# 32 columns of numerators: interleaved with the denominator sums, or in a round of their own

## The chip, the core and the metric

The kernel runs on one core of one Trainium2 chip. The core has a matrix engine (TensorE, PE in the profile, with its weight loads as PEld), a vector engine (VectorE, DVE), an activation engine (ScalarE, ACT), GpSimd (POOL) and SyncE (SP), each with an instruction queue of its own; they meet through semaphores. The metric is the device time of one execution in microseconds (us); lower is better. Times with two decimals in this document are starts within the span of the profiled execution.

## The reference

```python
def phi(x):                                     # per head, 8 x 8 products
    a = einsum('rd,bhsd->bhsr', S1, x)
    b = einsum('rd,bhsd->bhsr', S2, x)
    return einsum('bhsi,bhsj->bhsij', a, b).reshape(..., 64)
q_p, k_p = phi(q), phi(k)                       # q, k, v: 4 batches, 4 heads, 1088 tokens, 32 wide
kv  = einsum('bhsf,bhsd->bhfd', k_p, v)
z   = sum(k_p, axis=2)
num = einsum('bhsf,bhfd->bhsd', q_p, kv)
den = einsum('bhsf,bhf->bhs', q_p, z)[..., None] + 1e-06
x   = (num / den) as (4352 tokens, 128)
out = (sigmoid(x @ w_gate) * (x @ w_val)) @ w_out    # 1536 wide in between
```

All is float32. The attention part is linear in the tokens: each head needs one 64 x 32 matrix `kv` and one vector `z` of 64; then a numerator (32 values) and a denominator (one value) for each token.

## The kernel before, in words

**The feed-forward part is the long one.** The result of the attention lies in `xT`, 128 partitions (4 heads x 32) by 4352 tokens. The tokens are cut into eight chunks of 512 and a last one of 256. For each chunk `w1` makes twelve waves (`wave`, L544), each of 128 of the 1536 columns for gate and value; ScalarE takes the sigmoid (L552), VectorE multiplies (`glu`, L587), and the product with `w_out` follows some waves later as `prod` (L381), for which GpSimd makes sums of tokens (`tsum`, L371). For the chunks in the middle the weights are split in 64-column halves, so the profile shows those matmuls as 128*64.

**The attention of the batches 1 to 3 is slipped in between the waves.** The order on every engine is written out by hand. The function `slot` issues one wave and what has become due behind it; the list `plan` says at which wave each step of a batch stands. The steps of one batch are: transposes of k and q, features (`kps`, `qcomp`, `spread`, `outer`, `qmult`), `kv_all`, `ndt` (weights of the numerators, `ND`), `weights_z` (weights of the denominators, `ZW`), and last `parts(b)`, the step that this case is about. It stands in one slot for each of the three batches.

**The step `parts(b)`** does this:

1. `den_j` (L1026): eight matmuls `sum_j` (L1032), 64 rows by 32 columns of weights, 160 columns of data, into the PSUM tile `denj`. `pi` is the half of the rows (0 to 63, 64 to 127) and also the half of `denj`, which has two banks; `x` picks one of four groups of 32 output partitions. Between them stand eight numerator matmuls (L1268) of 32 columns, also into `denj`, columns 160 to 191. While `sum_j` uses the one half of the rows, the numerator beside it uses the other. Then VectorE multiplies `denj` by `A8` into `PD` (`pd`, L1047).
2. `glu()` for the wave before, on VectorE, behind `pd`.
3. The other 512 columns of numerators: eight matmuls (L1268) into the PSUM tile `nps`, copied to SBUF by ScalarE (`num`, L1285).
4. `den_i` (L1053): two matmuls of 128 rows by 64 columns on `PD`, back into columns 0 to 159 of the first bank of `denj`. They wait for `pd`.
5. `turn_den` and the rest on VectorE: transpose (`dTi`, L1065), reciprocal, transposes, and three multiplications into `xT` (L1302), the last of them of the 32 columns.

Each float32 matmul is two passes in the trace, each with its own weight load, so the eight 512-column matmuls are "x16". Tiles of 64 rows by 32 columns are eight separate parts of the array here, two halves of rows by four groups of columns.

The PSUM pool `ps2` has one buffer (tag "two"), two banks. `denj` lives in it, and so do `kps`, `kvz` and `ndps` of other steps: a new tile of that tag has to wait for all readers of the tile before it.

## Time and profile before

| | |
|---|---|
| median of 3 runs | 290.91 us (290.83 to 291.48) |
| profiled execution | 291.36 us, of which 289.3 us are the span of the instructions |
| granted TensorE clock | 1.0, all slices |
| TensorE busy | 283.5 us, 98% of the span |
| VectorE, GpSimd, ScalarE busy | 170.8, 159.6, 106.6 us |
| share of the chain that ended last on TensorE | 97% |
| first weight load of `parts(1)`, `parts(2)`, `parts(3)` | 72.44, 129.35, 193.57 us |

The 2.06 us between the span and the time of the execution lie around the instructions. The three steps `parts` look alike to 0.02 us in the trace, so the first stands for all. Ends of matmuls are modelled by the profiler: a matmul's duration contains the time in which its columns run in and the time in which the array empties, and the next one on the same part of the array starts before that end.

### The profile page before, as it was taken

Reading aid. Unit: us, or ns where it says so; the run is one execution under the profiler, and the core shown is the slowest. Engines: PE = TensorE matmul, PEld = TensorE weight load, DVE = VectorE, ACT = ScalarE, POOL = GpSimd, SP = SyncE. Lnnn points to the kernel's source line nnn. Section 1 sums busy time; section 2 is a strip of 40 time slices with the busy share of each in tenths; the row PEclk is TensorE's granted clock in tenths of the full one; section 3 lists DMA queues with packets and bytes.
Section 4 is the critical chain, followed back from the end, with each engine's and each line's share of the span. In section 5 each row is a group of like instructions: output and inputs, shape, how many; then the busy total and the mean of one; then the engine's idle time right before and its main releaser. Section 6 shows DMA issues by size and latency. Waiting matters only on the chain.

```text
span 289.3 us, 5786 instructions
## 1 busy us (share of the span) xinstructions
PE 283.5 (98%) x2260; PEld 134.9 (47%) x2260; DVE 170.8 (59%) x294; ACT 106.6 (37%) x215; POOL 159.6 (55%) x222
## 2 busy tenths in 40 slices
PE   8799999999999999999999999999999999999995
PEld 4454433354444444544444444444444444444685
DVE  6987788946738547668346385767245223522571
ACT  3688833222334322533234222522243223421341
POOL 2566673667466377372665396483564646555200
PEclk9999999999999999999999999999999999999999
DMA  7995541665600386442000683010001100020012
GB/s 216 343 361 120 111 155 42 164 147 135 186 11 2 77 187 162 105 156 37 0 1 6 157 162 128 2 28 10 0 3 18 18 2 0 3 35 1 0 17 40
DMA packets 28890, 24.22 MB, mean 84 GB/s; under 512 B 18560, under 2 KB 24064, under 8 KB 28864
## 3 DMA queue, kind: packets, MB, share of 16 engines
q1 hardware_dynamic: 25888, 22.10, 30.1%
q10 hardware_dynamic: 2976, 1.77, 2.1%
q8 instruction: 17, 0.28, 0.4%
q14 instruction: 9, 0.07, 0.1%
HBM read 20.60 MB, written 3.26 MB: 82 GB/s over the span
## 4 chain that ended last, share of the span: by engine, by line
PE 97%; ACT 1%; DVE 1%; issue 0%; POOL 0%
PE wave L544 61%; PE prod L381 22%; PE moeout L425 4%; PE moeout L451 2%; PE warm L301 2%; PE kvz L900 1%; PE nps L1268 1%; PE kps L681 1%; PE cqps L827 1%; PE nps L1101 0%; PE dps L1082 0%; PE denj L1053 0%; PE denj L1032 0%; ACT asb L798 0%; DVE qp L807 0%; PE ndps L965 0%
## 5 line engine op out<-in xcount | busy, mean ns | idle before, releaser
L544 PE MATMUL wave<-xT,w_sb 128*64 128x512 f32 (+3 forms) x820 | 201.9, 566 | 0.0
L552 ACT ACTIVATE sg<-wave 128x512 f32<-128x512 f32 x102 | 60.9, 597 | 158.6 <-PE wave L544 152.6
L587 DVE TENSOR_TENSOR g<-wave,sg 128x512 f32<-128x512 f32 x96 | 66.1, 688 | 88.2 <-ACT sg L552 87.6
L371 POOL TENSOR_TENSOR tsum<-g,tsum 128x256 f32<-128x256 f32 x84 | 68.4, 815 | 71.6 <-DVE g L587 71.5
L544 PEld LDWEIGHTS wave<-xT,w_sb 128*64 128x64 f32 (+1 forms) x820 | 71.3, 140 | 72.8 <-issue 53.0
L371 POOL TENSOR_TENSOR tsum<-g 128x256 f32<-128x256 f32 x84 | 66.4, 791 | 22.6 <-DVE g L587 22.0
L381 PE MATMUL prod<-tsum,ws 128*64 128x256 f32 x252 | 68.3, 380 | 0.0
L381 PE MATMUL prod<-g,w_sb 128*64 128x256 f32 x168 | 50.2, 380 | 0.0
L381 PEld LDWEIGHTS prod<-tsum,ws 128*64 128x64 f32 x252 | 34.0, 137 | 13.1 <-issue 9.7
L381 PEld LDWEIGHTS prod<-g,w_sb 128*64 128x64 f32 x168 | 22.7, 137 | 30.0 <-issue 25.8
L381 PE MATMUL prod<-tsum,w_sb 128*64 128x256 f32 x84 | 25.1, 380 | 0.0
L381 PE MATMUL prod<-g,ws 128*64 128x256 f32 x84 | 25.0, 379 | 0.0
L162 POOL TENSOR_TENSOR head<-head,tail 128x384 int32<-128x384 int32 (+1 forms) x13 | 13.2, 1021 | 4.4 <-DVE head L157 4.4
L381 PEld LDWEIGHTS prod<-g,ws 128*64 128x64 f32 x84 | 11.5, 137 | 5.7
L425 PE MATMUL moeout<-g,w_sb 128*128 128x512 f32 (+1 forms) x28 | 12.4, 600 | 0.0
L381 PEld LDWEIGHTS prod<-tsum,w_sb 128*64 128x64 f32 x84 | 11.3, 137 | 1.3 <-issue 1.0
L760 DVE TENSOR_TENSOR kp<-kab 128x1152 f32<-128x1152 f32 (+2 forms) x10 | 10.7, 1082 | 0.0
L580 DVE TENSOR_TENSOR g<-wave,sg 128x512 f32<-128x512 f32 x6 | 7.0, 1172 | 6.1 <-ACT sg L552 4.6
L880 DVE TENSOR_TENSOR qp<-qp,bq 128x1152 f32<-128x1152 f32 (+1 forms) x7 | 10.1, 1444 | 0.0
L493 DVE TENSOR_TENSOR res<-prod,other 128x256 f32<-128x256 f32 x14 | 6.0, 425 | 6.3 <-ACT other L484 4.8
L141 POOL TENSOR_SCALAR head<-cap 128x384 f32<-128x384 f32 (+1 forms) x13 | 6.3, 487 | 5.0 <-ACT cap L140 5.0
L152 ACT ACTIVATE tail<-w_in,two__157 128x384 f32<-128x384 uint32 (+1 forms) x12 | 7.3, 614 | 0.0
(132 smaller groups left out, 200.2 us busy)
## 6 DMA issues: line engine op xcount, KB each, us to landing
qp<-dq SPq DMA_DIRECT2D x7, 576.0 KB
bq<-dq SPq DMA_DIRECT2D x14, 288.0 KB
kq<-in_k_dram SPq DMA_DIRECT2D x3, 544.0 KB
kq<-in_q_dram SPq DMA_DIRECT2D x3, 544.0 KB
w_in<-in_moe_w_out_dram SPq DMA_DIRECT2D x6, 256.0 KB
w_in<-in_moe_w_gate_dram SPq DMA_DIRECT2D x5, 256.0 KB
w_in<-in_moe_w_val_dram SPq DMA_DIRECT2D x5, 256.0 KB
v<-in_v_dram SPq DMA_DIRECT2D x8, 144.0 KB
```

Source lines behind the costliest of these rows:

```text
L141: nc.gpsimd.tensor_scalar(out=self.head.bitcast(F32), in0=self.cap, scalar1=122880.0, scalar2=2.0**-15, op0=ALU.min, op1=ALU.max,)
L152: nc.scalar.activation(out=self.tail, in_=self.lo, func=ACTF.Identity, bias=two, scale=2.0**-51)
L162: nc.gpsimd.tensor_tensor(out=self.head, in0=self.head, in1=self.tail.bitcast(I32), op=ALU.add)
L371: nc.gpsimd.tensor_tensor(out=t[:, u], in0=in0, in1=in1, op=ALU.subtract)
L381: nc.tensor.matmul(out=out, lhsT=lhsT, rhs=rhs, start=start, stop=stop, skip_group_check=True)
L425: nc.tensor.matmul(out=moe["acc"][d], lhsT=w_sb[:, 2, j, d], rhs=g[:, jj], start=(j == 0), stop=(j == NJ - 1),)
L544: nc.tensor.matmul(out=wv[d, which, jj * tw + o : jj * tw + o + tp], lhsT=w_sb[:, which, j0 + jj, d], rhs=xT[:, t0 + o : t0 + o + tp], sta ...
L552: nc.scalar.activation(out=sg, in_=wv[:, 0], func=ACTF.Sigmoid)
L580: nc.vector.tensor_tensor(out=g.rearrange("p (j u s y) -> p j y u s", j=2, u=2, y=4), in0=wv[:, 1].rearrange("p (j y u s) -> p j y u s", j ...
L587: nc.vector.tensor_tensor(out=g, in0=wv[:, 1], in1=sg, op=MUL)
L760: eng.tensor_tensor(out=KP[b][:, pi, j0:j1].rearrange("p j m (i l) -> p (j m) i l", i=R), in0=bass.AP(tensor=a0.tensor, offset=a0.offset, ...
L880: nc.vector.tensor_tensor(out=q0, in0=q0, in1=half(BQ[b], n), op=MUL)
```

## The change

The 32-column numerators leave `den_j` and become a round of their own behind the 512-column ones. `den_j` is left with its eight `sum_j`. The function `numerators` issues all eight matmuls of one kind, in the order head, then half of the rows. In `parts` a new tile `nps2` of the tag "two" is taken after `den_j`; the 32-column numerators go to its columns 160 to 191, `den_i` to its columns 0 to 159, and `turn_den` and the last multiplication into `xT` read it in place of `denj`.

```diff
     def den_j(b):
         t = ps2.tile([P, 2, 512], F32, tag="two", name="denj")
-        rest = t[:, :, WD : WD + 32]
-        def sum_j(pi, x):
+        for pi in range(2):
             rows = slice(64 * pi, 64 * pi + 64)
-            nc.tensor.matmul(
-                out=t[32 * x : 32 * x + 32, pi, :WD],
...
-        for x in range(4):
-            sum_j(0, x)
-            numerator(b, rest, x, 1, True)
-        for x in range(4):
-            sum_j(1, x)
-            numerator(b, rest, x, 0, True)
+            for x in range(4):
+                nc.tensor.matmul(
+                    out=t[32 * x : 32 * x + 32, pi, :WD],
...
         nc.vector.tensor_tensor(out=PD[b], in0=t[:, :, :WD], in1=A8[b], op=MUL)
-        return t
...
+    def numerators(b, t, rest):
+        for h in range(H):
+            for c in range(2):
+                rows = slice(64 * c, 64 * c + 64)
+                q1 = QP[b].rearrange("p (n h w) -> p n h w", n=2, h=H)[rows, :, 2 * (h % 2) + h // 2]
+                nc.tensor.matmul(
+                    out=t[32 * h : 32 * h + 32, c],
+                    lhsT=ND[b][rows, 32 * h : 32 * h + 32],
+                    rhs=q1[:, 1, W1 - 32 :] if rest else q1[:, :, : W1 - 32],
...
     def parts(b):
-        t2 = den_j(b)
+        den_j(b)
         glu()
         t = psm.tile([P, 2, 512], F32, tag="wave", name="nps")
-        for h in range(H):
-            for c in range(2):
-                numerator(b, t, h, c, False)
+        numerators(b, t, False)
...
         nc.scalar.copy(out=num, in_=t)
-        turn_den(b, den_i(b, t2[:, 0, :WD]))
+        t = ps2.tile([P, 2, 512], F32, tag="two", name="nps2")
+        numerators(b, t[:, :, WD : WD + 32], True)
+        turn_den(b, den_i(b, t[:, 0, :WD]))
...
-            for u0, u1, x in ((0, 8, num[:, :, 256 * n : 256 * n + 256]), (8, tn, t2[:, :, WD : WD + 32])):
+            for u0, u1, x in ((0, 8, num[:, :, 256 * n : 256 * n + 256]), (8, tn, t[:, :, WD : WD + 32])):
```

In the program as built, TensorE has, per batch, 8 `sum_j`, 8 matmuls of 512 columns, 8 of 32 columns and the 2 of `den_i`, in this order; it had 8 `sum_j` and 8 of 32 columns alternating, 8 of 512 columns and the 2 of `den_i`. The wait for `pd` (VectorE) stands at the first 32-column matmul of `nps2`, where it stood at the first of `den_i`. No engine has an instruction more or less; the other engines' orders and every DMA are as they were.

More of the change, by code (lines that the diff above doesn't have):

```diff
@@ L1027, in den_j @@
         t = ps2.tile([P, 2, 512], F32, tag="two", name="denj")
-        rest = t[:, :, WD : WD + 32]
-        def sum_j(pi, x):
+        for pi in range(2):
             rows = slice(64 * pi, 64 * pi + 64)
-            nc.tensor.matmul(
-                out=t[32 * x : 32 * x + 32, pi, :WD],
-                lhsT=ZW[b][rows, 4 * (x % 2) : 4 * (x % 2) + 4].rearrange("p x i -> p (x i)"),
-                rhs=B8[b][rows, (W1 - WD) * (x // 2) : (W1 - WD) * (x // 2) + WD],
-                start=True,
-                stop=True,
-            )
-        for x in range(4):
-            sum_j(0, x)
-            numerator(b, rest, x, 1, True)
-        for x in range(4):
-            sum_j(1, x)
-            numerator(b, rest, x, 0, True)
+            for x in range(4):
+                nc.tensor.matmul(
+                    out=t[32 * x : 32 * x + 32, pi, :WD],
+                    lhsT=ZW[b][rows, 4 * (x % 2) : 4 * (x % 2) + 4].rearrange("p x i -> p (x i)"),
+                    rhs=B8[b][rows, (W1 - WD) * (x // 2) : (W1 - WD) * (x // 2) + WD],
+                    start=True,
+                    stop=True,
+                )
         PD[b] = sbA.tile([P, 2, WD], F32, tag="pd", name="pd", bufs=1)
         nc.vector.tensor_tensor(out=PD[b], in0=t[:, :, :WD], in1=A8[b], op=MUL)
-        return t
     def den_i(b, dps):
@@ L1263, in part01 @@
         late.append(dn(0, 1)(later=True))
-    def numerator(b, t, h, c, rest):
-        rows = slice(64 * c, 64 * c + 64)
-        q1 = QP[b].rearrange("p (n h w) -> p n h w", n=2, h=H)[rows, :, 2 * (h % 2) + h // 2]
-        nc.tensor.matmul(
-            out=t[32 * h : 32 * h + 32, c],
-            lhsT=ND[b][rows, 32 * h : 32 * h + 32],
-            rhs=q1[:, 1, W1 - 32 :] if rest else q1[:, :, : W1 - 32],
-            start=True,
-            stop=True,
-        )
+    def numerators(b, t, rest):
[7 more added lines that the diff above has]
+                    rhs=q1[:, 1, W1 - 32 :] if rest else q1[:, :, : W1 - 32],
+                    start=True,
+                    stop=True,
+                )
     def parts(b):
-        t2 = den_j(b)
+        den_j(b)
         glu()
         t = psm.tile([P, 2, 512], F32, tag="wave", name="nps")
-        for h in range(H):
-            for c in range(2):
-                numerator(b, t, h, c, False)
+        numerators(b, t, False)
         num = sbA.tile([P, 2, NJK, 2, F], F32, tag="kp", name="num", bufs=1)
```

## The prediction, made before the result was known

> **What bounds the kernel now.** I read first the page: busy times, the granted clock, and the chain of work that ended last.

> ```profile
> span 289.3 us, 5786 instructions
> ...
> PE 283.5 (98%) x2260; PEld 134.9 (47%) x2260; DVE 170.8 (59%) x294; ACT 106.6 (37%) x215; POOL 159.6 (55%) x222
> ...
> PEclk9999999999999999999999999999999999999999
> ...
> PE 97%; ACT 1%; DVE 1%; issue 0%; POOL 0%
> ```

> TensorE is busy in 98% of the span, the chain is TensorE for 97%, and its clock is granted in full. So a change of the end is, to first order, the change in the time that TensorE's own stream needs. Second, the chain between 70 and 80 us, in order of time (start, length, what).

> ```profile
> 70.79 1.72 PE wave L544 x8
> 72.51 0.18 PE denj L1032 x4
> ...
> 72.98 1.09 PE nps L1268 x16
> 74.07 0.42 PE denj L1053 x4
> 74.50 0.86 PE prod L381 x8
> 75.36 1.72 PE wave L544 x8
> ```

> From wave to prod nothing but TensorE: the step `parts` costs 1.99 us (72.51 to 74.50), three times 0.7% of the execution. Only what changes between the first `denj` pass and `prod` can count. Third, therefore, the timeline of that stretch (start, length, engine), asked for in narrow windows.

> ```profile
> 72.44 0.10 PEld L1032 LDWEIGHTS denj<-b,zw 64*32 64x32 f32 x1 [0.81 <-DMA v<-in_v_dram]
> 72.44 0.32 PE L1032 MATMUL denj<-b,zw 64*32 64x160 f32 x1
> ...
> 72.45 0.21 PE L1268 MATMUL denj<-qp,nd 64*32 64x32 f32 x1
> ...
> 72.80 0.59 PE L1268 MATMUL nps<-qp,nd 64*32 64x512 f32 x1
> ...
> 72.93 1.14 PE L1268 MATMUL nps<-qp,nd 64*32 64x512 f32 x15
> 73.21 0.49 DVE L1047 TENSOR_TENSOR pd<-denj,a 128x320 f32<-128x320 f32 x1 [1.83 <-PE denj L1032]
> ...
> 74.00 0.20 PEld L1053 LDWEIGHTS denj<-pd,head 128*64 128x64 f32 x4 [0.84 <-DVE pd L1047]
> ```

> The last line names `pd` as what `den_i` waited for. But `pd` ended at 73.21 + 0.49 = 73.70, and a TensorE load starts about 0.05 behind the VectorE instruction it waits for (`qT` ends at 14.18, the load of `cqps` starts at 14.23). From 73.75 on `pd` held nothing up. What did is the array: the last pass of `nps` has its modelled end at 74.07, and `den_i`, whose tile has another shape (128*64 after 64*32), loads 0.07 before it, just as the first `denj` load at 72.44 stands 0.07 before the modelled end of the wave (72.51). So `pd` has 0.25 us to spare now. The next answer, the second passes of `nps`, and one on all passes of `denj` give the durations:

> ```profile
> 73.23 0.84 PE L1268 MATMUL nps<-qp,nd 64*32 64x512 f32 x8
> ```

> ```profile
> L1032 PE MATMUL denj<-b,zw x48: 292/296/322, 72.4 to 193.9; 64*32 64x160 f32 x48
> ...
> L1268 PE MATMUL denj<-qp,nd x48: 188/193/214, 72.4 to 193.9; 64*32 64x32 f32 x48
> ```

> A pass of 512 columns lasts 0.59, one of 32 columns 0.19: 0.40 for 480 columns, 0.83 ns a column. So columns run for 0.43 (512), 0.13 (160) and 0.03 (32), and 0.16 of each duration is the array emptying. The last columns of `nps` are in at 74.07 - 0.16 = 73.91, and `den_i` follows 0.09 later. I follow the time of the last column before `den_i`, T = 73.91; the change in T, times three, is the change of the kernel.

> **The change, part by part.**

> *Front: 16 short passes leave `denj`.* Each of the eight parts of the array now takes two `sum_j` passes and two short ones. The first `nps` pass starts at 72.80 on the upper half of the rows; the other fifteen wait for the lower half until 72.93, and that sets T. On the lower half two short passes come first (72.45 and, 0.05 later, 72.50), then `sum_j` at 72.60 and 72.74 (0.13 of columns each), then `nps`. Without the short passes `sum_j` of the lower half can start at the earliest behind the four loads of the upper half, which come about 7 ns apart, two passes each: 72.47 to 72.50. Then `nps` gains 0.10 to 0.13. At the latest it starts at 72.60 as now, because its own wait (for the second half of `B8`, one of the two waits is a semaphore instruction of 0.05) or the second passes of the upper half (from 72.57) hold it: gain 0. A loss is possible as well: without the alternation the halves could run one after the other, and the lower half would start when the upper one's columns are in, 72.57 + 0.13 = 72.70: 0.10 later. The short passes did run beside `sum_j` of the other half in the trace, so parts of the array do start independently; I take a gain of 0.07, and keep -0.13 and +0.10 as ends.

> *Back: the 16 short passes stand behind `nps`.* They use the same eight parts and the same tile shape as `nps`, so there is no second emptying of the array between them. On the part that ends last, two more passes follow: 2 x 0.03 of columns, and the start of the first and of the second, 0.01 to 0.02 each (two short passes on one part stand 0.03 to 0.05 apart in `denj`). This is 0.06 at least and 0.10 at most, if the passes of the other parts run beside them, as the short passes of `denj` do at some 10 ns apart. A gain is excluded, since these columns can only come after `nps`. The far end: the round one pass after the other. The nearest row for that is `kvz`, 72 passes of 64 columns in 1.14 (the chain at 58.42): 0.016 each, 16 of them 0.25, and the first load, 0.10, not covered because it stands behind the wait for `pd`: 0.35. I take 0.09, near the `denj` row because that is the same tile shape with the same data, and keep 0.06 and 0.35.

> *The wait for `pd` moves ahead of the round.* Behind it on TensorE's queue stand the round, `den_i`, `prod` and the next wave. `pd` would be done at 73.70 as now, or up to 0.13 earlier with the front; the loads could start at 73.75. The part of the array that ends last is busy with `nps` until 73.91 - 0.07 = 73.84. So the wait is covered, by 0.09; the loads of the eight matmuls at 7 ns each use 0.05 of it. If `pd` came later than that, every 0.01 would cost 0.01 per batch. Cost taken: nothing, covered by the second passes of `nps`.

> *The tile `nps2`* waits for `pd` as the only reader of `denj`, the same wait. The next tile of the tag is needed only by the next batch's `kps`; after the last batch by the last chunk.

> *Other engines.* `num` (ScalarE) starts behind `nps`, so up to 0.07 earlier. `dTi` and the chain into `xT` move with `den_i`, by some 0.02. The last write to `xT` ends at 78.79; the first wave that reads these tokens starts at 79.92, its load at 79.71. That leaves 0.9 us. In batches 2 and 3 four waves lie between. POOL, SP and all DMAs keep their orders: nothing.

> *The sum.* Per batch -0.07 + 0.09 + 0 = +0.02, for three +0.06. The profiled execution, 289.3 + 2.06 around it = 291.36, becomes 291.42; it stands 0.45 above the median of the runs shown, so on the median: 290.97, rounded 291.0.

> [...]

> **The rivals.**

> *Slower: the round runs in series behind the wait.* If the first load of the round isn't covered (0.10) and its passes come at the pace of `kvz` (0.25), T is 0.35 - 0.07 = 0.28 later per batch, 0.84 in all: 291.75, or +0.29%. It decides from 0.19 per batch on. For it: nothing can be loaded ahead across the wait for `pd`, and the profile has no short round that stands alone. Against it: 32 short and long passes in 0.49.

> *Faster: the front is bound by the number of passes.* If `denj` is bound by passes and not by columns, half of the 32 passes is half of 0.49, so 0.25 per batch gained and 0.06 paid behind: -0.57 in all, 290.3. For it: the long and the short passes stand mixed at one pace. Against it: on the lower half the chain of starts accounts for no more than 0.13.

> *`pd` ends last.* It starts 0.14 behind the modelled end of the last `sum_j`, where `dTi` starts 0.05 behind `den_i`; so 0.09 are unexplained, perhaps its DMA waits. If that slack grew by 0.1 the cover would be gone: +0.1 per batch, 291.3; no change that can be told.

> That the round isn't placed where the change says can be left out: TensorE's order as built shows it.

> **How the numbers follow.** A measurement of this kernel can tell about 0.2% from no change, 0.58 us (its own runs spread from 290.83 to 291.48). The sum of my terms with nearer ends lies between -0.07 and +0.10 per batch, -0.2 and +0.3 in all, inside that bound. Chances: forecast 0.60 and `pd` last 0.08, both within 0.2%; in series 0.22, slower; bound by passes 0.10, faster. The far corner, halves in series in front and passes in series behind (+0.45 per batch, 292.3), is left out of the range, which reaches from the faster rival to the slower one, with 0.1 of each inside: 290.4 to 291.8. The forecast's own range is 290.6 to 291.4.

> **What would show it.** Right, if in the profile after: the first `den_i` load stands 1.50 to 1.65 us behind the first `denj` load (now 1.56); `nps`'s fifteen passes start 0.39 to 0.49 behind it; the short passes start within 0.15 and the first of them no later than 1.40 behind it; `pd` ends before the last `nps` columns are in. Wrong, if the first short load stands more than 0.1 behind both `pd` and the last columns of `nps`, if the short passes spread over 0.25, or if a wave waits for `xT`.

## The result, and the profile after

The changed kernel is a little faster, in the first comparison by 0.2 to 0.5%: 290.21 us (median of 14 runs, 290.00 to 290.75) beside 291.10 for the kernel before (14 runs on the same chip, 290.80 to 296.05). The ratio is 0.9965, with a 95% interval of 0.995 to 0.998; it is taken over fast executions alone, without the slow one of 296.05 us. A second comparison gave medians of 290.43 and 291.12 us and a ratio of 0.9987 (0.9973 to 1.000); the kernel before, run once more unchanged, gave 0.9994 (0.9984 to 1.0005). The forecast was a loss of 0.06 us.

First the page of the kernel after: span, busy times, shares of the chain that ended last.

```profile
span 288.4 us, 5785 instructions
...
PE 282.6 (98%) x2260; PEld 134.5 (47%) x2260; DVE 170.8 (59%) x294; ACT 106.6 (37%) x215; POOL 159.6 (55%) x222
...
PE 97%; DVE 1%; issue 0%; ACT 0%
```

TensorE is the bound as before, with 0.9 us less of busy time and a span 0.9 us shorter. The one instruction fewer (5786 before) is a wait for a semaphore in TensorE's stream. Then the chain of waits of the kernel after between 70 and 80 us (start, length, what).

```profile
70.43 1.72 PE wave L544 x8
72.14 0.43 PE denj L1029 x16
72.58 0.95 PE nps L1259 x27
73.53 0.42 PE nps L1042 x4
73.95 0.86 PE prod L381 x8
74.81 1.72 PE wave L544 x8
```

From the first `denj` to `prod` it is 73.95 - 72.14 = 1.81 us, where it was 1.99: 0.18 less. The wave, `prod` and the wave after it last what they lasted. The timeline of that stretch, in narrow windows (start, length, engine; buffer numbers are left out of names, so `nps` is also `nps2`; L1259 are the numerators, L1042 is `den_i`):

```profile
72.07 0.18 PEld L1029 LDWEIGHTS denj<-b,zw 64*32 64x32 f32 x16 [0.81 <-issue]
72.24 0.29 PEld L1259 LDWEIGHTS nps<-qp,nd 64*32 64x32 f32 x16
...
72.37 0.64 PE L1259 MATMUL nps<-qp,nd 64*32 64x512 f32 x8
...
72.69 0.49 DVE L1037 TENSOR_TENSOR pd<-denj,a 128x320 f32<-128x320 f32 x1 [1.67 <-PE denj L1029]
...
73.23 0.19 PEld L1259 LDWEIGHTS nps<-qp,nd 64*32 64x32 f32 x16 [0.70 <-DVE pd L1037]
73.46 0.20 PEld L1042 LDWEIGHTS nps<-pd,head 128*64 128x64 f32 x4
```

The eight first passes of the long numerators start together at 72.37, 0.30 behind the first load, within 0.05. Before, one started 0.36 behind the first load and the others from 0.49 on. The short round's loads stand at 73.23, and `den_i` follows at 73.46.

The step's length, from its first load to the first load of `den_i`, is the measure in all that follows, since it is alike to 0.002 us in all three batches: **1.562 us before, 1.382 after**. Three times 0.180 is 0.54 us, 0.19% of the execution. The spans differ by 0.9. The other 0.36 were there before the first wave: it starts at 14.53, and before at 14.90. In the kernel before, TensorE was slower at the start: the trace's record of the full clock begins at 6.58, after at 5.52, and the two warm-up matmuls of 128 columns, from 5.57 on, last 0.58 and 0.42, where after, from 5.52 on, they last 0.38 and 0.28. From the first wave to the end it is 274.403 us before and 273.870 after, and in a second profile of each 274.401 and 273.866. Of the 820 starts of wave passes in between, all keep their distances to 0.003, but at three places, the three steps, where the kernel after gains 0.18 each time. So in these profiles the 0.54 are all that the change does from the first wave on.

Over the profiles of this study the record of the full clock began between 3.69 and 6.86 and the first wave started between 14.33 and 15.17, with the same code in front of it. The two don't go in step: the latest first wave, 15.17, came with the full clock at 4.73. So the start of a single execution scatters by more than the change is worth, and the 0.36 are no effect of the change. The two comparisons differ in their medians by 0.89 and 0.69 us; 0.54 lies in the interval of the second and 0.04 outside that of the first. The median span, given to a tenth, was 289.0 in the 34 executions of the kernel before in the second comparison and 288.4 in the 26 of the kernel after: 0.6. What is left, up to 0.3 us, would have to lie in the time around the span (1.7 to 3.0 us in those executions); what causes it is not shown.

### The profile page after: what moved, and what is told of

It reads as the page before. It is cut to its first block, busy times and chain, and to the rows that moved or that the text cites. A ratio compares the mean times of both kernels' runs of the same rounds, so it can differ in the third digit from the quotient of the medians.

```text
span 288.4 us, 5785 instructions
## 1 busy us (share of the span) xinstructions
PE 282.6 (98%) x2260; PEld 134.5 (47%) x2260; DVE 170.8 (59%) x294; ACT 106.6 (37%) x215; POOL 159.6 (55%) x222
## 4 chain that ended last, share of the span: by engine, by line
PE 97%; DVE 1%; issue 0%; ACT 0%
PE wave L544 61%; PE prod L381 22%; PE moeout L425 4%; PE moeout L451 2%; PE warm L301 2%; PE kvz L900 1%; PE nps L1259 1%; PE kps L681 1%; PE cqps L827 1%; PE nps L1090 0%; PE denj L1029 0%; PE dps L1071 0%; PE nps L1042 0%; PE gram L704 0%; DVE qp L807 0%
## 5 line engine op out<-in xcount | busy, mean ns | idle before, releaser
L544 PE MATMUL wave<-xT,w_sb 128*64 128x512 f32 (+3 forms) x820 | 201.9, 565 | 0.0
L544 PEld LDWEIGHTS wave<-xT,w_sb 128*64 128x64 f32 (+1 forms) x820 | 71.2, 140 | 72.8 <-issue 53.0
L381 PE MATMUL prod<-tsum,ws 128*64 128x256 f32 x252 | 68.2, 380 | 0.0
L381 PE MATMUL prod<-g,w_sb 128*64 128x256 f32 x168 | 50.2, 380 | 0.0
L381 PEld LDWEIGHTS prod<-tsum,ws 128*64 128x64 f32 x252 | 34.0, 137 | 13.1 <-issue 9.7
L381 PEld LDWEIGHTS prod<-g,w_sb 128*64 128x64 f32 x168 | 22.7, 137 | 30.0 <-issue 25.8
L381 PE MATMUL prod<-tsum,w_sb 128*64 128x256 f32 x84 | 25.0, 380 | 0.0
L381 PE MATMUL prod<-g,ws 128*64 128x256 f32 x84 | 25.0, 379 | 0.0
L381 PEld LDWEIGHTS prod<-g,ws 128*64 128x64 f32 x84 | 11.5, 137 | 5.7
L381 PEld LDWEIGHTS prod<-tsum,w_sb 128*64 128x64 f32 x84 | 11.3, 137 | 1.3 <-issue 1.0
```

What stands on the lines that cost most here:

```text
L381: nc.tensor.matmul(out=out, lhsT=lhsT, rhs=rhs, start=start, stop=stop, skip_group_check=True)
L544: nc.tensor.matmul(out=wv[d, which, jj * tw + o : jj * tw + o + tp], lhsT=w_sb[:, which, j0 + jj, d], rhs=xT[:, t0 + o : t0 + o + tp], sta ...
```

## The experiments

Where the experiments were single runs, their times tell little for the reason just given; the step's length tells what each edit did. (The profiles of two of them are about 1 us longer in a place that the edit doesn't touch: "same half" between 16 and 20 us, "two heads" behind the last wave.) Three ideas were to be told apart. **Alternation**: the two kinds of matmul hinder each other because they stand mixed. **Number**: it counts how many matmuls stand ahead of the long ones, whatever their kind and order. **Halves of the rows**: the chain of starts on one half of the array, as in the prediction. All starts below, in us behind the step's first load, are read from the single records of the trace of the first batch:

```
kernel              ahead of   first passes of the eight long matmuls           step
                    them
before              16   .358 | .493 .510 .526 .543 .559 .576 .593     1.562
after                8   .298   .304 .311 .318 .324 .331 .338 .344     1.382
shorts between      16   .358 | .493 .509 .526 .543 .559 .576 .593     1.561
shorts first        16   .408   .432 .439 .452 .539 .571 .578 .585     1.531
no shorts            8   .297   .304 .310 .317 .324 .330 .337 .344     1.290
two heads           12   .349 .358 .364 .384 .391 | .493 .509 .526     1.555
sums twice          16   .569   .576 .582 .589 .596 .602 .609 .616     1.654
one head first      16   .361 .367 .412 | .556 .572 .589 .606 .623     1.592
```

The bar stands where a start is late without a reason on its own part of the array.

**The short matmuls between the sums and the long ones** (kernel after, edited):

```diff
 def den_j(b):                  # behind the eight sums
...
+    numerators(b, t[:, :, WD : WD + 32], True)
...
+    return t
...
 def parts(b):
-    den_j(b)
+    t2 = den_j(b)
...
-    t = ps2.tile([P, 2, 512], F32, tag="two", name="nps2")
-    numerators(b, t[:, :, WD : WD + 32], True)
-    turn_den(b, den_i(b, t[:, 0, :WD]))
+    turn_den(b, den_i(b, t2[:, 0, :WD]))
```

> The eight short matmuls (32 columns) stand in a row between the eight sum_j and the eight of 512 columns, in the tile denj, so there is no second tile and no wait for pd ahead of them. Measured from the first weight load of the step to the first load of den_i, per batch: 1.56 us in the kernel before, 1.39 in the changed one. Theory A (the alternation of long and short passes keeps the weight loads from running ahead; the passes themselves cost little): 1.30 for sums and nps plus 0.06 to 0.09 for a round of short passes, 1.36 to 1.39; the sixteen nps loads come about 7 ns apart. Theory B (the front is bound by the number of passes ahead of nps, wherever they stand): 1.56, as before.

Timeline of this kernel, TensorE's passes (L1261 are the numerators of both kinds):

```profile
72.49 0.50 PE L1029 MATMUL denj<-b,zw 64*32 64x160 f32 x16
72.78 0.25 PE L1261 MATMUL denj<-qp,nd 64*32 64x32 f32 x13
72.84 0.59 PE L1261 MATMUL nps<-qp,nd 64*32 64x512 f32 x1
...
72.98 0.71 PE L1261 MATMUL nps<-qp,nd 64*32 64x512 f32 x7
```

One long pass starts at 72.84, the other seven only from 72.98, and every one of the eight stands where it stood in the kernel before. Nothing alternates here. **Alternation falls**: the gain does not come from taking the two kinds apart. **Halves of the rows** doesn't explain the gap either: with the sums in one row, the parts of the array are free early (the last short pass starts at 0.373, its 32 columns run for 0.03), and the seven are still late.

**The short matmuls first**: the same, but with the `numerators` line ahead of the eight sums.

> The eight short matmuls stand in a row ahead of the eight sum_j, in the tile denj. Theory A (alternation): first load of the step to first load of den_i 1.36 to 1.39 us, nps starts 7 ns apart. Theory B (number of passes): 1.56. If a wait for data of the short matmuls (qp, nd) or of the sums (b8) comes to light here, the step's start moves instead.

The step was 1.531 (290.58 us, beside 291.39 for the kernel before). There is no gap behind the first long pass. But the sums themselves came late: waits for semaphores are instructions of their own in TensorE's stream, each 0.051 and then some 0.025 up to the next load (in the kernel before one lasts from 0.023 to 0.074, and the next load stands at 0.099), and three of them stand within the first 0.35, two ahead of the sums and one ahead of the long numerators. In the kernel after, the two ahead of the sums are passed 2 to 3 us earlier, while the waves ahead still run; in the kernel before, one of them is. So this order most likely loses at the waits most of what it gains at the gap, and does not separate the ideas cleanly.

**The short matmuls on the same half as the sum beside them** (kernel before, edited):

```diff
         for x in range(4):
             sum_j(0, x)
-            numerator(b, rest, x, 1, True)
+            numerator(b, rest, x, 0, True)
         for x in range(4):
             sum_j(1, x)
-            numerator(b, rest, x, 0, True)
+            numerator(b, rest, x, 1, True)
```

> As in the kernel before, each sum_j is followed by a short matmul, but on the same half of the rows (sum_j of rows 0 to 63 with the numerator of rows 0 to 63, and so on), so on each part of the array a long one is followed by its short one. First load of the step to first load of den_i: theory A, if any alternation of long and short is what hurts: 1.56 us as before. Theory A', if it is the alternation between the halves: 1.36 to 1.39. Theory B (number of passes): 1.56. Together with e2_between this tells B from A.

Timeline of this kernel's passes:

```profile
73.39 0.59 PE L1268 MATMUL nps<-qp,nd 64*32 64x512 f32 x1
...
73.55 0.73 PE L1268 MATMUL nps<-qp,nd 64*32 64x512 f32 x7
```

Again one long pass alone and a gap of 0.16 (0.36 and 0.51 behind the first load); the step is 1.605, 0.04 longer than before. The load behind the gap stands at 73.52 in the trace (in the view of the weight loads: start, length, engine), 0.49 behind the first load as in the kernel before:

```profile
73.52 0.28 PEld L1268 LDWEIGHTS nps<-qp,nd 64*32 64x32 f32 x14
```

So the gap is the same, whichever half the short ones use. A second, smaller gap follows: the third long pass comes only at 0.554, where it was 0.510 before. That is the 0.04, and it is taken up again below.

**No short matmuls at all** (kernel after, edited; the 32 columns are not computed):

```diff
-        numerators(b, t[:, :, WD : WD + 32], True)
...
-            ... (8, tn, t[:, :, WD : WD + 32])):
+            ... (8, tn, num[:, :, 0:32])):
```

> The short matmuls are left out altogether: the last 64 tokens of batches 1 to 3 get other columns' numerators, so the computation of these tokens is left out. The rest is the changed kernel. First load of the step to first load of den_i: 1.30 us by both theories (1.39 less the 0.09 of the round behind nps). If the wait for pd, not the passes, sets the changed kernel's 1.39, it stays above 1.30, because den_i then waits for pd itself: pd ends 1.11 behind the first load, and den_i could load at 1.16 at the earliest, so the array's emptying at 1.30 should decide. Prices: the round behind nps is the difference to 1.39, the front the difference to 1.56.

Timeline of the weight loads:

```profile
72.71 0.18 PEld L1029 LDWEIGHTS denj<-b,zw 64*32 64x32 f32 x16 [0.81 <-issue]
72.87 0.29 PEld L1259 LDWEIGHTS nps<-qp,nd 64*32 64x32 f32 x16
74.00 0.20 PEld L1042 LDWEIGHTS nps<-pd,head 128*64 128x64 f32 x4 [0.84 <-DVE pd L1037]
```

From 72.71 to 74.00, 1.290 exactly, is the step without the round. With it: behind the long ones 1.382, **0.092 more**; mixed in ahead of them 1.562, **0.272 more**. These are the two prices that the prediction had at 0.09 and 0.07 (the second as a gain). The last line says that `den_i` waited for `pd`, though `pd` had ended 0.19 earlier (1.103 behind the step's start); what held it was the array, as in the profile before: its load stands 0.09 behind the last long column in both.

**The eight sums twice** (kernel after; the whole loop of sums issued once more ahead of it, into columns 192 to 351), so that 16 matmuls stand ahead of the long ones and none of them is short:

```diff
+        for pi in range(2):
+            ...                  # the eight sums, out=t[32 * x : 32 * x + 32, pi, 192 : 192 + WD]
```

> The changed kernel with its eight sum_j issued twice (the first time into columns of denj that nobody reads), so that 16 matmuls with long passes stand ahead of nps and no short one. The second eight keep each part of the array busy for 2 x 0.13 longer, so nps would start at 0.30 + 0.27 = 0.57 and den_i's load stand at 1.38 + 0.27 = 1.65 us behind the step's first load. Theory S (what holds nps up in the kernel before is that its matmuls follow short ones): 1.65, the nps starts 7 ns apart. Theory Q (the number of matmuls that TensorE's sequencer has ready when the step begins is about 16; the next ones come at the sequencer's own pace): the second nps start stands 0.13 behind the first, the others 16 ns apart, and den_i 1.75 to 1.90.

Passes of this kernel (L1029 and L1039 the two rounds of sums):

```profile
72.61 0.32 PE L1029 MATMUL denj<-b,zw 64*32 64x160 f32 x4
72.71 0.48 PE L1039 MATMUL denj<-b,zw 64*32 64x160 f32 x16
72.99 0.64 PE L1269 MATMUL nps<-qp,nd 64*32 64x512 f32 x8
```

Sixteen matmuls ahead, and the eight long passes start together, 0.007 apart. So a number alone, with a fixed price for each matmul, **falls too**. What is different here? Sixteen long matmuls ahead take so long that the first one has left the array before the second long numerator is due (0.49 against 0.58). This leads to the idea that explains the gaps in the table.

**The limit.** At every bar of the table **17 float32 matmuls are begun and not yet through**. The 18th is loaded no earlier than 0.031 us after the modelled end of the first one's second pass, and where the limit holds several in a row, each comes 16.5 ns behind the one ahead and not 6.6. In the kernel before: the first sum's second pass starts at 0.162 and lasts 0.296, its end and 0.031 make 0.489, and the load of the second long matmul, the 18th of the step, stands at 0.489:

```profile
72.93 0.23 PEld L1268 LDWEIGHTS nps<-qp,nd 64*32 64x32 f32 x14
```

With the sums twice it is there too, in the loads: the second long numerator is loaded at 0.488 (0.458 + 0.031 = 0.489), though its own part was ready for the load at 0.442, and the next ones 16.5 ns apart; only the passes are too late to show it. In "same half" the second matmul is a short one that waits for the first sum on its own part; its second pass ends at 0.518, and the 19th matmul, the third long one, is loaded at 0.549. With the short ones first, the first matmul leaves so early that the limit is never felt, and that row has no bar. The limit says where the bar must stand when fewer or other matmuls are ahead.

**Two heads ahead, two behind** (kernel after; `numerators` takes a list of heads):

```diff
 def den_j(b):                  # behind the eight sums
...
+    numerators(b, t[:, :, WD : WD + 32], True, (0, 1))
...
 def parts(b):                  # behind the eight long ones, t = t2
...
+    numerators(b, t[:, :, WD : WD + 32], True, (2, 3))
```

> The short matmuls of heads 0 and 1 stand between the sums and nps, those of heads 2 and 3 behind nps; all in denj. Ahead of nps stand 12 matmuls. Theory S (short ones right ahead of nps): the second nps start stands 0.13 behind the first, den_i's load at about 1.50 us. Theory P (a part of the array takes a third matmul only when its second has begun, and everything behind it in order waits): the same place, since the parts of heads 0 and 1 are the first of nps. Theory Q (about 16 ready): the first four nps starts are 7 ns apart and the gap of 0.13 stands at the fifth; den_i at about 1.50.

Twelve matmuls are ahead, so the 18th is the sixth long one; there the gap is, 0.391 to 0.493, with its load at 0.489 again. The step is 1.555. Half of the short ones are gone from the front, but the last long second pass starts only 0.07 earlier (0.977; 1.044 before, 0.774 after), where a price for each matmul would have made it half of 0.27.

**One head of short matmuls first, the sums, then the other three heads** (16 ahead of the long ones):

```diff
 def den_j(b):
...
+    numerators(b, t[:, :, WD : WD + 32], True, (0,))       # ahead of the sums
     ...
+    numerators(b, t[:, :, WD : WD + 32], True, (1, 2, 3))  # behind them
```

> The two short matmuls of head 0 stand ahead of the sums, the six others between the sums and nps, all in denj: 16 matmuls ahead of nps, as in the kernel before. Theory R: TensorE has at most 17 matmuls begun; the 18th is loaded only when the first has left the array (0.03 behind its modelled end). Here the first two are short and have left by 0.3, the third is a sum_j that leaves at about 0.50. So the second and third nps start early (by 0.45 at the latest) and the gap stands ahead of the fourth, at 0.50 to 0.53, then 16 ns each. Theory Q (the first 17 are ready when the step begins, and the rest comes when the sequencer has caught up, whatever has left): the gap stands ahead of the second nps again, at 0.49.

R is the limit just told; it was stated before this run, from those told so far. The first two matmuls are short now and leave early, the third is the first sum. Passes of this kernel (L1262 the numerators):

```profile
72.30 0.59 PE L1262 MATMUL nps<-qp,nd 64*32 64x512 f32 x2
72.31 0.21 PE L1262 MATMUL denj<-qp,nd 64*32 64x32 f32 x3
72.35 0.82 PE L1262 MATMUL nps<-qp,nd 64*32 64x512 f32 x6
```

The first load behind the gap:

```profile
72.49 0.20 PEld L1262 LDWEIGHTS nps<-qp,nd 64*32 64x32 f32 x10
```

Three long passes start early (0.361, 0.367, 0.412), and the gap stands ahead of the fourth, which is the 20th matmul: its load waits for the third to leave. The third's second pass starts at 0.225; with 0.296 and 0.031 that makes 0.552, and the load stands at 0.552. The 18th, waiting for the first short one (second pass 0.053, with 0.193 and 0.031: 0.277), is loaded at 0.278. The gap came a little later than the 0.50 to 0.53 of the expectation, since the first sum itself began later, behind the short matmul on its own part. So the limit is **shown**, by its place and to 0.001 us; theory Q, with the gap ahead of the second long pass, falls.

**The round behind issued twice** (kernel after; once more into columns 192 to 223):

```diff
+        numerators(b, t[:, :, WD + 32 : WD + 64], True)
         numerators(b, t[:, :, WD : WD + 32], True)
```

> The changed kernel with its round of short matmuls behind nps issued twice (the first into columns that nobody reads). First load of the step to first load of den_i 1.38 us in the changed kernel, 1.29 without a round. If a round costs its passes (7 ns each, 16 passes, 0.10): 1.46 to 1.49. If the 0.09 are mostly the wait for pd and the start of the round: 1.41 to 1.43.

Timeline of the weight loads:

```profile
72.23 0.18 PEld L1029 LDWEIGHTS denj<-b,zw 64*32 64x32 f32 x16 [0.81 <-issue]
72.39 0.29 PEld L1259 LDWEIGHTS nps<-qp,nd 64*32 64x32 f32 x16
73.39 0.44 PEld L1259 LDWEIGHTS nps<-qp,nd 64*32 64x32 f32 x32 [0.70 <-DVE pd L1037]
73.86 0.20 PEld L1042 LDWEIGHTS nps<-pd,head 128*64 128x64 f32 x4
```

The step is 1.633, 0.251 more for a second round that was expected to cost about as much as the first, 0.092. It is the limit once more: counted from the first long matmul (8 long, 8 short, 8 short) the 18th is the second of the second round. Its load is due at 0.727 + 0.589 + 0.031 = 1.347 and stands at 1.348. The first round is free of this by one matmul: 8 long and 8 short are 16.

**A later `pd`** (kernel after; a copy of 64 columns on VectorE ahead of `pd`):

```diff
+        late_pd = sbA.tile([P, 2, 32], F32, tag="latepd", name="latepd", bufs=1)
+        nc.vector.tensor_copy(out=late_pd, in_=t[:, :, :32])
         nc.vector.tensor_tensor(out=PD[b], in0=t[:, :, :WD], in1=A8[b], op=MUL)
```

> The changed kernel with one more VectorE instruction (a copy of 64 columns out of denj, about 0.2 us) ahead of pd, so that pd ends about 0.15 to 0.2 later. In the changed kernel the round's first load stands 0.05 behind pd's end and also just where the first nps passes end (1.16). If the wait for pd is covered no more, den_i's load comes later by the full delay: 1.53 to 1.58 us. If there is cover left as I predicted (0.09): 1.45 to 1.50.

Timeline of VectorE and of the loads of this kernel:

```profile
73.22 0.23 DVE L1037 COPY latepd<-denj 128x64 f32<-128x64 f32 x1 [1.68 <-PE denj L1029]
73.40 0.49 DVE L1039 TENSOR_TENSOR pd<-denj,a 128x320 f32<-128x320 f32 x1
...
74.01 0.21 PEld L1261 LDWEIGHTS nps<-qp,nd 64*32 64x32 f32 x16 [0.94 <-PE denj L1029]
74.26 0.20 PEld L1044 LDWEIGHTS nps<-pd,head 128*64 128x64 f32 x4
```

`pd` ends 0.177 later, and `den_i` is loaded 0.268 later (step 1.650), more than either expectation. The first load of the round stands 0.115 behind the end of `pd` instead of 0.052, and its first pass 0.146 instead of 0.054: with the extra reader of `denj` there is a wait instruction of its own behind `pd` (0.051 long), which costs about 0.09. Both delays together make the 0.268, so the delay passes on in full. In the kernel after, the wait for `pd` has **no cover left**: the load stands at 1.156, 0.052 behind the end of `pd`, and in the same moment the first part of the array has taken its last long column (0.727 + 0.43 = 1.157).

An order with the round behind the long ones, but without its wait for `pd`, wasn't tried: in `denj` the short matmuls wait for `pd` as well (with two heads behind, their first load stands at 1.248, 0.053 behind its end), and a tile elsewhere would be needed. No order was found that is shorter than 1.382.

## Why the prediction was wrong

**Front: wrong in size; this is the step that failed.** "16 short passes leave `denj`" was taken as a gain of 0.07 for each batch with an end at 0.13; it measured 0.27 (1.562 against 1.290 without them). The prediction looked only at when the parts of the array come free. That chain is there, and it gave its end and not its middle: on the part of the last long matmul, the last sum pass starts at 0.335 before, so its columns are in at 0.335 + 0.13 = 0.47, and after, that long matmul starts at 0.344: 0.13. But before it did not start at 0.47. The limit of 17 held the second long pass until 0.493 and let the six behind it come 16.5 ns apart instead of 6.6, so the last one started at 0.593 (0.12 more), and the second passes follow their first ones at 0.451 instead of 0.430 (0.02). 0.13 + 0.12 + 0.02 = 0.27. Eight matmuls fewer ahead of the long ones took away both bounds. Taking away the chain alone brings nothing, as the kernel with the short ones between showed; taking away the limit alone wasn't tried. Two rows spoke for the limit beforehand: the pass at 72.93, 0.493 behind the first load, stands 0.09 behind the last column on its part, and the prediction's "the other fifteen wait for the lower half until 72.93" took no notice of that (it read that part's sum passes as 72.60 and 72.74; they start at 72.57 and 72.70, so its columns are in 0.266 + 0.13 = 0.40 behind the first load); and the seven first passes behind the gap come at more than twice the 7 ns that the prediction itself had read in `denj`. The 0.49 that it gave to the 32 passes of `denj` (72.44 to 72.93) holds the gap as well: the last of them starts at 0.37.

**Back: right.** 0.09 predicted, 0.092 measured. The 16 short passes start within 0.104, and within 0.10 where they stand in a row ahead of the sums. The eight long first passes of the kernel after, on separate parts of the array, start 6.6 ns apart (0.298 to 0.344).

**The wait for `pd`: right in its price, wrong in its margin.** No cost of it can be read at the round's first load, but with the front gain as it came out, long columns and `pd` end in the same moment. The cover of 0.09 belonged to a front gain of 0.07; had `pd` not moved forward with the sums (it ends 0.16 earlier, since they are through in 0.21 and not in 0.34), the round would have been held, by an estimate, until 1.263 + 0.05 = 1.31 instead of 1.156, and most of the gain would have been lost. This was the rival "`pd` ends last"; it came to a tie.

**`den_i` waits for the array, not for `pd`: right.** Before, after and without the round it is loaded 0.09 behind the last column. **Other engines and `xT`: right**: no wave waited (the wave passes keep their distances outside the three steps).

**The rivals.** The slower one, the round in series, did not come: 0.092 and not 0.35. The faster one, "bound by the number of passes", 0.25 gained and 0.06 paid, was near in size (0.272 and 0.092) and is wrong in its reason: with all sixteen long matmuls ahead the passes start without a gap, and half of the short ones gone brought a quarter of the gain. So of the signs given, `den_i` at 1.50 to 1.65 (1.38) and the fifteen passes at 0.39 to 0.49 (0.30 to 0.34, the eight first ones) failed; the three on the round and `pd` held.

**What is not shown.** Why it is 17 that are begun when the next one is held, and why the ones behind come 16.5 ns apart. No run here counted matmuls of another type or outside this step.

## What to carry to other kernels

In this step eight small float32 matmuls on separate parts of the array cost 0.092 behind the long ones, where no more than 17 were begun before the first had left, and 0.251 as a second round, where the count ran over. In a like step look, for each matmul, at when the one 17 places ahead of it leaves, and put short ones where the count does not run over in front of long ones. A start that is late without a wait and without a busy part is a reason to look for such a limit, before the gain of an edit is bounded by the parts alone. A wait that moves with a gain has to be costed anew at the new time, not at the old one.
